# The output's store gets a semaphore of its own, awaited behind the context's closing, and sends 128 rows in place of 32

## The chip, the cores and the metric

The kernel runs on one core of one Trainium2 chip. The metric is the device time of one execution in microseconds (us). A profiled execution gives, beside its own time, a span: the time from the first to the last instruction of the program.

## The reference

One decode step (one token for each of two batch rows, D = 512) of a transformer block with adaptive layer norm:

```python
mod = (silu(c) @ w_mod)                  # six vectors sa, ca, ga, sb, cb, gb
h = layernorm(x) * (1 + ca) + sa
x = x + ga * attention(h)                # 32 heads of 128, caches K and V of 4096 rows each
h = layernorm(x) * (1 + cb) + sb
x = x + gb * mish_ffn(h)                 # 512 -> 1376 -> 512, Mish between
return x                                 # float32, 2 x 1 x 512
```

Everything is float32. The two caches are 2 x 32 x 4096 x 128 each, 134 MB a piece; with the weights the core reads 297 MB from HBM in one execution. The result is 4 KB.

## The kernel before

**The stream.** All that is read in bulk passes through three buffers called `room` (64 KB on each of 128 partitions). `stream()` (line 31) fixes by hand what each fill holds: for most fills one head of K and one head of V, with the pieces of `wq`, `wo` and the modulation weights fitted between. `load(n)` (line 134) issues the DMAs of fill n at line 141, all on the SyncE queue (SP in the profile); `used(...)` (line 146) calls it as soon as the buffer of fill n-3 is no longer needed. There are 45 such DMAs, in program order, and each SP instruction waits on semaphores for the buffer that it overwrites.

**The heads.** For every head VectorE multiplies K with the broadcast query (line 318), sums over the head dimension (line 321) and takes a row maximum; ScalarE makes the exponentials (line 337); TensorE sums V with those weights (line 359) and projects (line 390).

**The end.** After the last head come the second layer norm, the two layers of the feed-forward part (lines 514 and 556), the scaling with the last modulation vector (line 564), and the residual (line 565), whose result stands in the tile `y`, 128 partitions of 128 floats. Only eight of the 128 rows of `y` are part of the answer: every sixteenth row; the rest is padding that the matmul layout leaves. Line 566 stores every fourth row, 32 rows of 512 bytes, to the DRAM tensor `out`, as the last DMA of the SP queue:

```python
y = work.tile([P, P], F32, tag="sq", name="y", bufs=1)
nc.vector.tensor_tensor(out=y, in0=yps[:, :P], in1=mod[5], op=ALU.mult)
nc.vector.tensor_tensor(out=y, in0=y, in1=x2, op=ALU.add)
nc.sync.dma_start(out=out, in_=y[::OUT_STEP, :])
```

**The closing.** The kernel is built inside a `tile.TileContext` (line 636), which assigns the semaphores. When the context ends, it adds a closing of its own, whose instructions the profile files under line 636. SP waits, in six small semaphore instructions, for the full count of every semaphore that the context gave out: those of the DMAs (eight of them, taken in turn by all DMAs, the store too), and one of each engine. Then SP drains; all five engines meet at a barrier that POOL (GpSimd) leads; POOL drains and clears the context's semaphores; a second barrier follows, and the program of the kernel is over. The barriers use two semaphores that are not the context's.

The host takes every fourth of the 32 rows (line 639).

Of the kernel before, what the change touches and what calls it, by code (L numbers as in the profile page):

```python
# [8 lines left out]
F32 = mybir.dt.float32  # L9
# [4 lines left out]
P = 128  # L14
# [8 lines left out]
    "k": BIG, "v": HALF, "wq": W, "wo": W, "m01": 2 * W, "m2": W, "m3": W, "m4": W, "m5": W,  # L23
    "w1": 4 * sum(WIDTHS), "w2": 512 * len(CHUNKS),
}
OUT_STEP = 4
AHEAD = (14, 22)
ROW = 2 * BIG

# [40 lines left out]
def kernel(  # L70
# [3 lines left out]
    head: bass.AP,  # L74
    b1c: bass.AP,
    out: bass.AP,
):


# [6 lines left out]
    nc = tc.nc  # L86
# [16 lines left out]
    work = ctx.enter_context(tc.tile_pool(name="work", bufs=2))  # L103
# [42 lines left out]
    def used(*keys):  # L146
# [24 lines left out]
        out=fold, in_=ident.rearrange("p (g r) -> p r g", g=G), axis=AX.X, op=ALU.add  # L171
# [3 lines left out]
        out=mean_w, in0=fold[:, None, :].to_broadcast([P, G, R]), scalar1=1.0 / D, scalar2=None, op0=ALU.mult  # L175
# [4 lines left out]
        out=half, in_=ident.rearrange("p (b r) -> p r b", b=B), axis=AX.X, op=ALU.add  # L180
# [373 lines left out]
    for n in range(NCH):  # L554
        for t in range(G):
# [4 lines left out]
                start=(n == 0),  # L560
                stop=(n == NCH - 1),
            )
    y = work.tile([P, P], F32, tag="sq", name="y", bufs=1)
    nc.vector.tensor_tensor(out=y, in0=yps[:, :P], in1=mod[5], op=ALU.mult)  # L564
    nc.vector.tensor_tensor(out=y, in0=y, in1=x2, op=ALU.add)
    nc.sync.dma_start(out=out, in_=y[::OUT_STEP, :])


def _lay_out(np, a):
# [70 lines left out]
```

## Time and profile before

| | |
|---|---|
| time before, median of 3 runs | 698.54 us (698.48 to 698.58) |
| the profiled execution's own time | 698.42 us |
| its span, first to last instruction | 696.6 us |
| mean granted TensorE clock | 0.676 |
| VectorE (DVE) busy | 587.7 us, 84% of the span |
| TensorE (PE) busy | 283.8 us, 41% |
| read from HBM, written | 297.22 MB, 0.02 MB |
| mean rate of the DMA engines | 427 GB/s |

How to read it: the page names instructions by line of the kernel and engine, and tiles as output<-input. A `q` after an engine (SPq, POOLq) is its sequencer, which issues DMAs and handles semaphores; such instructions are not counted as busy time. Where a semaphore instruction waits, its row begins only when the wait is over. The chain of waits follows the work that ended last back from the last instruction; it ends at the last instruction that does work, and the closing and the store's flight are not in it. Times in the rows of the timeline are the start, in us from the span's start, and the duration.

### The profile page before, as it was taken

The page shows a single profiled execution, that of the slowest core. Times are in us where ns is not written, and L with a number is a line of the kernel's source. Part 1 is how long each engine was busy: PE and PEld are TensorE (multiplying, and loading weights), DVE is VectorE, ACT ScalarE, POOL GpSimd, SP SyncE. Part 2 cuts the span into 40 slices and gives each one's busy share as a digit, 9 for nine tenths or more (in the row PEclk, how much of TensorE's full clock was granted, in tenths as well). Part 3 has the DMA queues.
Part 4 walks back from the last instruction along what each step waited for, and adds up shares of the span by engine and source line. Part 5 has one row for each costly group of instructions (what it writes and reads, how often), then busy time and mean ns, then how long its engine had stood idle before and what let it go on. Part 6 is the DMA issues. An engine that isn't in the chain of part 4 may idle for free.

```text
span 696.6 us, 3912 instructions
## 1 busy us (share of the span) xinstructions
PE 283.8 (41%) x1636; PEld 102.4 (15%) x1636; DVE 587.7 (84%) x220; ACT 44.0 (6%) x168; POOL 4.2 (1%) x19
## 2 busy tenths in 40 slices
PE   3403334335245615335232806234333526224686
PEld 1200001001011201102100301011101101001234
DVE  3799899999999999999999999999999999899002
ACT  1000000000000000000000000000000000000010
POOL 2000000000000000000000000000000000000000
PEclk9855666667566665656585756666575657555789
DMA  9999999999999999999999999999999999999996
GB/s 392 452 421 421 426 474 421 419 429 421 467 422 425 429 425 456 429 425 426 433 448 429 426 429 437 440 430 429 433 437 437 429 425 422 452 427 420 423 422 270
DMA packets 6706, 297.49 MB, mean 427 GB/s; under 512 B 888, under 2 KB 928, under 8 KB 1184
## 3 DMA queue, kind: packets, MB, share of 16 engines
q1 hardware_dynamic: 6528, 297.23, 98.9%
q8 instruction: 13, 0.21, 0.1%
q10 hardware_dynamic: 160, 0.01, 0.0%
q14 instruction: 5, 0.04, 0.0%
HBM read 297.22 MB, written 0.02 MB: 427 GB/s over the span
## 4 chain that ended last, share of the span: by engine, by line
DMA 69%; DVE 28%; PE 2%; issue 0%; SPq 0%; ACT 0%; DVEq 0%
DMA room<-in_load 69%; DVE room L318 14%; DVE s L321 14%; PE ov L359 1%; PE qps L291 1%; PE modps L247 1%; PE yps L556 0%; SPq L141 0%; DVE m L334 0%; DVE hcw L280 0%; ACT q L292 0%; PE hps L237 0%; DVE y L564 0%; DVE hq L270 0%; DVE hq L271 0%
## 5 line engine op out<-in xcount | busy, mean ns | idle before, releaser
L318 DVE TENSOR_TENSOR room<-room,q 128x8192 f32<-128x8192 f32 x32 | 278.2, 8692 | 46.8 <-DMA room<-in_load 42.4
L321 DVE TENSOR_REDUCE s<-room 128x64 f32<-128x8192 f32 x32 | 277.9, 8683 | 0.4 <-DVE m L334 0.3
L359 PE MATMUL ov<-room,e 128*32 128x512 f32 x1024 | 176.4, 842 | 80.1 <-ACT e L337 63.9
L330 PE MATMUL mt<-d,same 128*128 128x64 f32 x64 | 18.2, 378 | 195.8 <-DVE d L328 195.8
L359 PEld LDWEIGHTS ov<-room,e 128*32 128x32 f32 x1024 | 39.2, 145 | 188.6 <-issue 133.8
L337 ACT ACTIVATE e<-s,m 64x64 f32<-64x64 f32 x64 | 22.1, 345 | 556.6 <-DVE m L334 555.8
L330 PEld LDWEIGHTS mt<-d,same 128*128 128x128 f32 x64 | 13.1, 254 | 225.8 <-DVE d L328 179.3
L291 PE MATMUL qps<-room,hcw 128*128 128x512 f32 x64 | 43.4, 844 | 4.8 <-DMA room<-in_load 4.0
L345 PE MATMUL l<-l,ones 128*128 128x8 f32 x16 | 4.6, 358 | 75.1 <-ACT e L337 75.1
L382 PE MATMUL otp<-pick,o 128*128 128x8 f32 (+2 forms) x72 | 13.4, 313 | 33.9 <-ACT o L374 32.0
L291 PEld LDWEIGHTS qps<-room,hcw 128*128 128x128 f32 x64 | 16.8, 274 | 26.4 <-issue 20.5
L374 DVE COPY o<-ov 128x256 f32<-128x256 f32 x1 | 0.4, 425 | 22.6 <-ACT o L374 22.6
L382 PEld LDWEIGHTS otp<-pick,o 128*128 128x128 f32 x72 | 12.6, 263 | 42.3 <-ACT o L374 39.4
L345 PEld LDWEIGHTS l<-l,ones 128*128 128x128 f32 x16 | 3.8, 296 | 76.5 <-ACT e L337 76.5
L334 DVE TENSOR_REDUCE m<-mt 128x1 f32<-128x64 f32 x32 | 6.9, 217 | 7.6 <-PE mt L330 7.6
L390 PE MATMUL att<-room,ot 128*32 128x512 f32 x62 | 10.1, 709 | 5.2 <-DMA room<-in_load 4.7
L337 ACT ACTIVATION_READ_ACCUMULATOR e<-s,m 64x1 f32 x64 | 11.8, 185 | 0.0
L328 DVE TENSOR_SCALAR d<-half,m 128x64 f32<-128x64 f32 x32 | 8.1, 254 | 1.1
L247 PE MATMUL modps<-room,ct 128*32 128x128 f32 (+1 forms) x160 | 8.1, 346 | 2.3 <-DMA room<-in_load 2.2
L326 DVE TENSOR_REDUCE m<-s 128x1 f32<-128x64 f32 x32 | 7.0, 217 | 0.9
L374 ACT COPY o<-ov 128x512 f32<-128x512 f32 (+1 forms) x9 | 5.0, 561 | 25.9 <-PE ov L359 25.7
L247 PEld LDWEIGHTS modps<-room,ct 128*32 128x32 f32 x160 | 5.0, 121 | 4.6 <-issue 4.4
(101 smaller groups left out, 60.6 us busy)
## 6 DMA issues: line engine op xcount, KB each, us to landing
room<-in_load SPq DMA_DIRECT2D x4, 4096.0 KB, 25.0
room<-in_load SPq DMA_DIRECT2D x1, 7168.0 KB, 39.1
room<-in_load SPq DMA_DIRECT2D x1, 3072.0 KB, 26.2
room<-in_load SPq DMA_DIRECT2D x3, 1024.0 KB, 28.3
room<-in_load SPq DMA_DIRECT2D x1, 2400.0 KB
room<-in_load SPq DMA_DIRECT2D x1, 2304.0 KB, 20.4
room<-in_load SPq DMA_DIRECT2D x1, 1376.0 KB, 15.8
room<-in_load SPq DMA_DIRECT2D x2, 256.0 KB, 22.8
```

What stands on the lines that cost most here:

```text
L247: nc.tensor.matmul(ps[R * g : R * (g + 1)], lhsT=ct[:, k, :], rhs=t[:, k, :].rearrange("p (m n) -> p m n", m=n)[:, :, P * g : P * (g + 1)] ...
L291: nc.tensor.matmul(ps, lhsT=hcw[:, k, :], rhs=wq_t[ch][:, k, :], start=(k == 0), stop=(k == G - 1))
L318: nc.vector.tensor_tensor(out=k_t[h], in0=k_t[h], in1=qv, op=ALU.mult)
L321: nc.vector.tensor_reduce(out=s_t[h], in_=k_t[h], axis=AX.X, op=ALU.add)
L326: nc.vector.tensor_reduce(out=m_t[h][:, 0:1], in_=s_t[h], axis=AX.X, op=ALU.max)
L328: nc.vector.tensor_scalar(out=d, in0=half, scalar1=m_t[h][:, 0:1], scalar2=None, op0=ALU.mult)
L330: nc.tensor.matmul(mps[h], lhsT=same, rhs=d, start=True, stop=True)
L337: nc.scalar.activation(e_t[i][own_b, :, M * i + 4 * b : M * i + 4 * b + 4], s_t[h][own_b].rearrange("p (c m) -> p c m", m=4), AF.Exp, bias ...
L345: nc.tensor.matmul(lps[n], lhsT=ones, rhs=sum_t[n % 2], start=True, stop=True)
L359: nc.tensor.matmul(ov[bank][R * g : R * (g + 1), :], lhsT=e_t[h % HC][:, NB // 2 * part + c, :], rhs=v_t[h, part][:, c, :], start=(first a ...
L382: nc.tensor.matmul(tps[:, x], lhsT=o_t[m], rhs=pick_t[n][:, m, x], start=(m == 0), stop=(m == 3),)
L390: nc.tensor.matmul(att[R * i : R * (i + 1), :], lhsT=ot_t[n % 2][:, i, :], rhs=wo_t[n][:, i, :], start=(n == 0), stop=(n == H // HC - (2 i ...
```

## The change

`OUT_STEP` goes from 4 to 1, so the store sends all 128 rows of `y` (64 KB in place of 16 KB, 128 rows of 512 bytes in place of 32), and the DRAM tensor `out` has 128 rows. The host takes every sixteenth.

The store adds to a semaphore `out_done` that is allocated outside of the context. Its name is put into `no_tile_sem_insts`, so the context neither counts it on one of its own semaphores nor waits for it. Behind the context's closing, SP waits until `out_done` has its 16 counts, and clears it.

`y` is allocated outside of the context's pools, since it is read after the context's last wait; it no longer shares the buffer of the tag `sq`.

```diff
-OUT_STEP = 4
+OUT_STEP = 1
...
+    out_done,
+    y,
...
-    y = work.tile([P, P], F32, tag="sq", name="y", bufs=1)
     nc.vector.tensor_tensor(out=y, in0=yps[:, :P], in1=mod[5], op=ALU.mult)
     nc.vector.tensor_tensor(out=y, in0=y, in1=x2, op=ALU.add)
-    nc.sync.dma_start(out=out, in_=y[::OUT_STEP, :])
+    store = nc.sync.dma_start(out=out, in_=y[::OUT_STEP, :]).then_inc(out_done, 16)
+    tc.no_tile_sem_insts.add(store.ins.name)
...
+    args["out_done"] = nc.alloc_semaphore("out_done")
+    args["y"] = nc.alloc_sbuf_tensor("y", [P, P], F32).ap()
     with tile.TileContext(nc) as tc:
         tile_adaln_decode_kernel(tc, **args)
+    nc.sync.wait_ge(args["out_done"], 16)
+    nc.sync.sem_clear(args["out_done"])
```

In the program as it is built, every engine has the same instructions in the same order as before, but for SP: the store waits for VectorE alone (before, it also waited for the DMA that had used its semaphore last), and one instruction stands behind the closing, which waits for `out_done` and clears it. One more thing differs there: each of the 45 loads carries a mark of the build for a prepared form of DMA (`ant_dge_precooked`), which the store of 32 rows with a stride of four lacked and the store of 128 rows has. All 201 SBUF tiles but five stand 512 bytes higher on each partition, because `y` lies below them.

## The prediction

> **What bounds the kernel now.** I read the page first (span, slices, chain), then the chain in order of time, then the rows of the stretch that the change touches: the last 3 us.
>
> ```profile
> span 696.6 us, 3912 instructions
> DMA  9999999999999999999999999999999999999996
> DMA room<-in_load 69%; DVE room L318 14%; DVE s L321 14%; PE ov L359 1%; PE qps L291 1%; PE modps L247 1%; PE yps L556 0%; SPq L141 0%; DVE m L334 0%; DVE hcw L280 0%; ACT q L292 0%; PE hps L237 0%; DVE y L564 0%; DVE hq L270 0%; DVE hq L271 0%
> ```
>
> The DMA engines are busy in every slice but the last, and the stream's loads hold 69% of the chain. The reader is to see two things: the time is set by a stream that the diff does not edit, and the store (line 566) is not even named in the chain. So a gain can come only from what follows the last arithmetic. That end, from four views (timeline, SP's instructions of line 566 and of 636, SP's waits):
>
> ```profile
> 693.74 0.29 DVE L565 TENSOR_TENSOR y<-y,x 128x128 f32<-128x128 f32 x1
> 694.06 0.55 SPq L566 DMA_DIRECT2D out<-y  x1
> L566 SPq DMA_DIRECT2D out<-y x1: 547/547/547, 694.1 to 694.1; - x1
> out<-y SPq DMA_DIRECT2D x1, 16.0 KB, 1.7
> ...
> L636 SPq EVENT_SEMAPHORE  x5: 17/28/28, 694.7 to 694.9; - x5
> L636 SPq EVENT_SEMAPHORE  x1: 27/27/27, 695.8 to 695.8; - x1
> L636 POOLq EVENT_SEMAPHORE_RANGE_CLEAR  x1: 96/96/96, 696.2 to 696.2; - x1
> L636 PEldq EVENT_SEMAPHORE  x1: 51/51/51, 696.6 to 696.6; - x1
> ...
> SPq L636 <- DMA out<-y: 0.9, 1, 0.9
> SPq L636 <- PEq L636: 0.6, 2, 0.4
> ```
>
> The store is issued at 694.06 and lands 1.7 us later, at 695.8. Of the closing's six semaphore instructions on SP five pass at once, at 694.7 to 694.9, and the sixth stands for 0.9 us until the store has landed (its row starts when the wait is over). Only then come the two barriers and POOL's clearing, and the last instruction of all is PE leaving the second barrier at 696.6. The flight is cut up by a view of the DMA packets and by one of stretches:
>
> ```profile
> GB/s 0 0 26 154 128 103 103 103 103 77 0 26 0 0 0 0 0 0 0 0 0 0 0 0 0 0 0 0 0 0 0 0 0 0 0 0 0 0 0 0
> DMA packets 48, 0.02 MB, mean 21 GB/s; under 512 B 16, under 2 KB 48, under 8 KB 48
> ...
> 694.60:695.25 0.65, 0.00 (x0) 0.00 (x0) 0.00 (x0) 0.00 (x0) 0.00 (x0) 1.00 0.00 0
> 695.25:695.46 0.21, 0.00 (x0) 0.00 (x0) 0.00 (x0) 0.00 (x0) 0.00 (x0) 1.00 0.30 78
> 695.46:695.80 0.34, 0.00 (x0) 0.00 (x0) 0.00 (x0) 0.00 (x0) 0.00 (x0) 1.00 0.00 0
> 695.80:696.63 0.83, 0.00 (x0) 0.00 (x0) 0.00 (x0) 0.00 (x0) 0.00 (x0) 0.69 0.00 0
> ```
>
> The first row has 40 slices of 0.02 us from 695.2. So the end before is a sum: issue 0.55 (to 694.61), silence 0.64 (to 695.25), packets 0.21 (32 with data and 16 of under 512 B, which are the counts), silence 0.34 until the counts are in (695.80), closing 0.83 (to 696.63).
>
> **The change part by part.**
>
> *The closing goes beside the flight.* In the built program the store adds to `out_done` alone, so all six of SP's semaphore instructions pass at once. The five took from 694.61 (the issue's end) to 694.93, 0.32 us; the rest of the closing takes 0.83 from the sixth on, as before. That work is not shortened; it is hidden beside the flight as long as the flight is longer.
>
> *The issue.* The 32-row store took 547 ns to issue. The built program marks the 128-row store as it marks the loads, so the nearest rows are the loads' issues, and, for the same two kinds on the other queue, ScalarE's two:
>
> ```profile
> L141 SPq DMA_DIRECT2D room<-in_load x31: 327/328/428, 118.9 to 643.9; - x31
> 1.07 1.15 ACTq L161 DMA_DIRECT2D cx<-in_head  x1
> 2.26 0.36 ACTq L164 DMA_DIRECT2D bias<-in_b1c  x1
> ```
>
> A marked load that waited takes 327 or 328 ns, one that follows another up to 428. On ScalarE the unmarked DMA (8 rows) took 1.15, the marked one (128 rows) 0.36. The store waits for VectorE, so I take 0.33: issue end at 694.06 + 0.33 = 694.39, a gain of 0.22. The bounds are 0.33 and, if the mark does nothing, 0.55.
>
> *The flight.* I keep the silence of 0.64 after the issue; the very first load, on an idle queue, agrees:
>
> ```profile
> 0.73 0.39 SPq L141 DMA_DIRECT2D room<-in_load  x1
> DMA  0000000099999009009090990000000000000009
> DMA packets 14, 0.46 MB, mean 573 GB/s; under 512 B 0, under 2 KB 0, under 8 KB 0
> ```
>
> Its issue ended at 1.12, and in this row (slices of 0.02 us from 1.6) the first packet is at 1.76: 0.64 again. So the first packet of the new store is at 695.03. Then it has 128 data packets in place of 32, eight in place of two on each of 16 engines. No row shows such a store, so I bound it from both sides. Low: in the stretch of 0.21 us the engines were busy 0.30 of it, 0.30 x 0.21 x 16 = 1.01 us of engine time, at most 1.01 / 32 = 0.032 us per data packet, so six more in file on an engine add 0.19. Nothing makes it less, since bytes and packets only grow. High: the 16 engines might start late one after the other, as in the load above, whose 14 first packets are spread over 0.6 us; then the last engine starts at +0.6 and needs 8 x 0.032 = 0.26, together 0.86 in place of 0.21, that is +0.65. The store's own 16 engines started closely (in the first five slices of its row), so I take a value near the low end, +0.25. The silence of 0.34 until the counts are in stays: landing at 695.03 + 0.21 + 0.25 + 0.34 = 695.83, about where it was. The shorter issue pays for the added rows.
>
> The Trainium skill, "DMA: Bandwidth & Descriptors", section "Anatomy of one DMA", puts a DMA at some 2.0 us fixed, mostly the write's receipt, plus bytes over 436e9 per second; by that the added 48 KB would be an estimated 0.11 us, and the sum 0.14 us better than mine. It speaks for the low end; the trace's flight of 1.7 us is somewhat shorter than its constant. The same page's section "Bandwidth", under "Measured", speaks against the change: about 10.5 ns a packet for a transfer of small packets, by which 96 more would be an estimated 1.0 us, and all of the gain would be lost (the second rival has this outcome). This trace does not agree with that rate: 48 packets went in 0.21 us, 4.4 ns each.
>
> *The wait behind the closing.* SP is through the closing at 694.39 + 0.32 + 0.83 = 695.54, and the other engines too, 0.29 before the landing. The wait then holds SP until 695.83. Behind it on SP stands only the clearing, and no engine waits for that. Its price: before, SP's own semaphore row took 0.03, and POOL's clearing 0.10, so 0.13 at most and 0.02 at least; I take 0.13. End of the span: 695.96. If the flight were shorter than expected, the cover of 0.29 would be gone and the closing would set the end, at 695.54, so the span cannot fall by more than about 1.0 us here.
>
> *The rest.* The wait of the store for an older DMA goes:
>
> ```profile
> SPq L566 <- DMA room<-in_load: 1.4, 1, 1.4
> SPq L566 <- DVE y L565: 22.2, 1, 22.2
> ```
>
> It was over 22.2 us before the store could start, so it costs nothing either way. `y` outside of the pools removes no instruction and no wait on VectorE, whose order is unchanged; lines 564 and 565 keep 0.29 each. The other edits are on the host or only move tiles by 512 bytes.
>
> *The sum.* Span: 696.63 - 695.96 = 0.67 us less; with the ends of the transfer 0.73 and 0.27. Around the span lie 698.42 - 696.6 = 1.8 us that no row shows. If what comes after the program starts when the last engine (now SP) is through, they stay: 0. If an engine other than SP is the slow one there, it now starts up to 696.63 - 695.54 = 1.09 earlier rather than 0.67: up to 0.42 more. I take 0.1, nearer to none. In all 0.77 against the profiled 698.42, that is 697.65; the median of the runs shown is 0.12 higher, so 697.77 against it, rounded **697.8**.
>
> **The rivals.**
>
> 1. *The store's wait is not moved, only doubled.* If the context still awaited the store, the closing would stay behind the landing (695.83 + 0.83) and the new wait would add 0.13: 696.79, +0.16, about 698.7. Against it: in the built program the store has left the context's semaphores, and SP's closing has no count for it. For it: the rows of before show only that the wait exists.
>
> 2. *The landing is late; the wait behind the closing takes the place of the one removed.* This one ends slower than before. It decides from the point where the landing passes 696.63 - 0.13 = 696.50, that is, when the flight after the shorter issue grows by over 0.92 us (695.58 would be the landing without added rows). Price: if the silence of 0.34 us before the counts are in grew with the data, four times as long, it would add 1.02, with 0.19 for the packets 1.21: landing at 696.79, end at 696.92, +0.29, about 698.8. For it: the silence is longer than the packets themselves, so something other than the packets sets it. Against it: every engine's packets go out together, and one silence followed all 32.
>
> 3. *The stream pays for the moved tiles.* With nearly every tile 512 bytes higher and a larger output in DRAM, the loads may run at another rate, either way. The stream is 69% of 696.6, 481 us, and its rate is not the same everywhere:
>
> ```profile
> 160.00:260.00 100.00, 42.48 (x180) 13.33 (x178) 92.90 (x28) 6.32 (x24) 0.00 (x0) 0.65 1.00 434
> 460.00:560.00 100.00, 41.97 (x184) 15.70 (x188) 93.00 (x28) 6.93 (x26) 0.00 (x0) 0.64 1.00 432
> ```
>
> A step from 434 to 432 GB/s, 0.46%, over 481 us is 2.2 us: about 700.0 the one way, 695.6 the other. It makes the kernel slower than before from a loss of 0.77 / 481 = 0.16%. For it: the engines are full (share 1.00), so nothing would hide it. Against it: neither the sizes of the loads nor their order changes, and 434 and 432 stand in one execution with fixed tiles, so that difference has another cause.
>
> 4. *More falls than the span shows*: the other engines' earlier end shortens what follows the program by the whole 0.42, and the transfer is at its low end: 0.73 + 0.36 = 1.09 (the floor of the other engines' gain), about 697.4.
>
> **How the numbers follow.** Forecast (697.5 to 698.4) 0.78; rival 4 (697.3 to 697.5) 0.10; rival 1 at 698.7 0.02; rival 2 at 698.8 0.05; rival 3 0.05, split 0.03 slower and 0.02 faster. The range goes from the largest gain, 1.1, with the runs' own spread of 0.1, to the smallest, 0.27, with the same spread: 697.3 to 698.4. It leaves out rivals 1 to 3, 0.12. A measurement of this kernel can tell about 0.2% from no change, 1.4 us; the forecast and rivals 1, 2 and 4 lie within it, so same 0.95, faster 0.02, slower 0.03.
>
> **What would show each step.** Right: SP's issue of the store at about 330 ns; SP's six semaphore rows of the closing all within some 0.4 us of it; POOL's clearing at 695.2, ahead of the landing; 144 packets on the store's queue from about 695.0; landing 1.7 to 1.8 us after the issue starts; SP's last instruction, not PE's, ending the span at about 696.0, and the stream's rows unchanged to 0.1 us. Wrong: an issue of 550 ns (the mark does nothing, 0.22 less gain); first packets spread over more than 0.3 us or a silence longer than 0.34 (rival 2, in whole or in part); the closing still behind the landing (rival 1); a start of line 565 off 693.74 by over 0.3 us (rival 3); a time outside of the span other than 1.8 us (rival 4).

## The result and the profile after

The changed kernel takes 697.59 us in the median (22 runs, 697.27 to 697.79). The kernel before, run beside it, takes 698.63 (22 runs, 698.36 to 699.03). The ratio is 0.9985 with a 95% interval of 0.9979 to 0.9991. That is 1.04 us or 0.15% faster: less than the 0.2% below which the prediction calls two times the same, but the interval does not reach 1, so the gain is real. The profiled execution takes 697.51 us, its span is 695.7.

The end of the changed kernel in the timeline:

```profile
693.47 0.29 DVE L565 TENSOR_TENSOR y<-yps,mod 128x128 f32<-128x128 f32 x1 [2.78 <-PE yps L558]
693.79 0.29 DVE L566 TENSOR_TENSOR y<-y,x 128x128 f32<-128x128 f32 x1
694.11 0.34 SPq L567 DMA_DIRECT2D out<-y  x1
```

The last addition starts at 693.79 in place of 693.74, so to 0.05 us the stream has neither gained nor lost in these two executions. The issue is down from 0.55 to 0.34. Then SP's waits, in which the 0.9 for the store is gone:

```profile
SPq L567 <- DVE y L566: 23.5, 1, 23.5
SPq L640 <- PEq L640: 0.6, 2, 0.4
```

The instructions of the closing (line 640 here) in three of its stretches: its six semaphore instructions, POOL's clearing, the last barrier.

```profile
L640 SPq EVENT_SEMAPHORE  x6: 17/28/28, 694.5 to 694.8; - x6
...
L640 POOLq EVENT_SEMAPHORE_RANGE_CLEAR  x1: 96/96/96, 695.2 to 695.2; - x1
...
L640 POOLq EVENT_SEMAPHORE  x2: 17/17/17, 695.4 to 695.5; - x2
...
L640 PEldq EVENT_SEMAPHORE  x1: 51/51/51, 695.6 to 695.6; - x1
```

All six pass at once, at 694.5 to 694.8, and POOL clears at 695.2 in place of 696.2. PE leaves the last barrier at 695.6 in place of 696.6. The new instruction behind the closing:

```profile
L643 SPq EVENT_SEMAPHORE_RANGE_CLEAR  x1: 25/25/25, 695.7 to 695.7; - x1
```

And the flight, cut at the issue's end (694.45), the first and last packet and the landing:

```profile
694.45:694.94 0.49, 0.00 (x0) 0.00 (x0) 0.00 (x0) 0.00 (x0) 0.00 (x0) 1.00 0.00 0
694.94:695.30 0.36, 0.00 (x0) 0.00 (x0) 0.00 (x0) 0.00 (x0) 0.00 (x0) 1.00 0.62 182
695.30:695.66 0.36, 0.00 (x0) 0.00 (x0) 0.00 (x0) 0.00 (x0) 0.00 (x0) 1.00 0.00 0
```

The reader is to see that the landing has hardly moved, 695.8 before and 695.66 now, with four times the data, while the closing has moved from behind it to beside it: it ends within 0.1 us of the landing.

**The table of all runs.** The "tail" is the profiled execution's own time less the start of its last addition (the row `y<-y,x`), which takes the stream's differences between executions out. SP and POOL "through" are the starts of their last rows in the span.

| kernel | median us | before beside it | ratio, 95% interval | tail us | POOL through | SP through |
|---|---|---|---|---|---|---|
| before | 698.63 | | | 4.68 | 696.5 | 696.6 |
| changed | 697.59 | 698.63 | 0.9985 (0.9979 to 0.9991) | 3.72 | 695.5 | 695.7 |
| own_sem_32rows | 697.88 | 698.65 | 0.9988 (0.9979 to 0.9997) | 3.82 | 695.7 | 695.9 |
| rows128_only | 698.32 | 698.65 | 0.9995 (0.9986 to 1.0004) | 4.47 | 696.8 | 696.9 |
| y_moved_only | 698.58 | 698.65 | 0.9998 (0.9989 to 1.0007) | 4.79 | 696.6 | 696.7 |
| own_sem_32_contiguous | 697.65 | 698.65 | 0.9985 (0.9976 to 0.9993) | 3.75 | 695.6 | 695.7 |
| four_copies | 698.42 | 698.67 | 0.9997 (0.9988 to 1.0006) | 4.41 | 696.0 | 697.0 |
| eight_copies | 699.16 | 698.67 | 1.0008 (0.9999 to 1.0016) | 5.24 | 695.9 | 697.8 |
| wait_on_pool | 697.68 | 698.67 | 0.9987 (0.9978 to 0.9996) | 3.84 | 696.1 | 695.9 |
| store_on_act | 697.31 | 698.67 | 0.9981 (0.9973 to 0.9990) | 3.43 | 695.6 | 696.1 |
| eight_copies_pool | 699.79 | 698.57 | 1.0018 (1.0009 to 1.0027) | 5.80 | 697.7 | 695.8 |
| changed_again | 697.58 | 698.57 | 0.9985 (0.9976 to 0.9994) | 3.60 | 695.8 | 695.9 |
| store_on_act_again | 697.26 | 698.57 | 0.9981 (0.9972 to 0.9990) | 3.45 | 695.3 | 695.7 |

The tails of one kernel differ by about 0.1 us between executions (changed 3.72 and 3.60; before and y_moved_only, whose ends are alike, 4.68 and 4.79). What lies outside of the span, the time less the span, is on average over the runs 1.83 us in before, 1.76 in changed, 1.75 in own_sem_32rows, 1.38 in four_copies, 1.36 in eight_copies, 1.87 in wait_on_pool, 1.89 in eight_copies_pool, and 1.46 and 1.47 in the two of store_on_act.

### The profile page after: what moved, and what is told of

It is laid out like the page before. It is cut to its first block, busy times and chain, and to the rows that moved or that the text cites. A ratio compares the mean times of both kernels' runs of the same rounds, so it can differ in the third digit from the quotient of the medians.

```text
span 695.7 us, 3912 instructions
## 1 busy us (share of the span) xinstructions
PE 284.7 (41%) x1636; PEld 103.9 (15%) x1636; DVE 587.5 (84%) x220; ACT 44.0 (6%) x168; POOL 4.2 (1%) x19
## 2 busy tenths in 40 slices
DMA packets 6802, 297.54 MB, mean 428 GB/s; under 512 B 888, under 2 KB 1024, under 8 KB 1280
## 4 chain that ended last, share of the span: by engine, by line
DMA 69%; DVE 28%; PE 3%; issue 0%; SPq 0%; ACT 0%; DVEq 0%
DMA room<-in_load 69%; DVE room L320 14%; DVE s L323 14%; PE qps L293 1%; PE ov L361 1%; PE modps L249 1%; PE yps L558 0%; SPq L143 0%; DVE m L336 0%; DVE hcw L282 0%; PE hps L239 0%; ACT q L294 0%; DVE hq L272 0%; DVE hq L273 0%; DVE y L565 0%
## 5 line engine op out<-in xcount | busy, mean ns | idle before, releaser
L361 PE MATMUL ov<-room,e 128*32 128x512 f32 x1024 | 174.1, 832 | 74.2 <-ACT e L339 40.4
L293 PE MATMUL qps<-room,hcw 128*128 128x512 f32 x64 | 46.1, 891 | 4.8 <-DMA room<-in_load 4.0
L294 ACT ACTIVATE q<-qps 128x512 f32<-128x512 f32 x8 | 4.8, 597 | 15.9 <-PE qps L293 15.7
```

What stands on the lines that cost most here:

```text
L293: nc.tensor.matmul(ps, lhsT=hcw[:, k, :], rhs=wq_t[ch][:, k, :], start=(k == 0), stop=(k == G - 1))
L361: nc.tensor.matmul(ov[bank][R * g : R * (g + 1), :], lhsT=e_t[h % HC][:, NB // 2 * part + c, :], rhs=v_t[h, part][:, c, :], start=(first a ...
```

## The experiments

Theory 1: the gain is the closing that now goes beside the flight; the time follows the end of the closing, and SP's wait behind it is covered by something on another engine after the program. Theory 2: the time follows the landing and SP's last instruction. Rival 3: the gain lies in the store's form, not in the semaphore.

### The parts alone

The changed kernel with

```diff
-OUT_STEP = 1
+OUT_STEP = 4
```

> The semaphore of its own and the wait behind the closing alone; the store keeps 32 rows with a stride of four (OUT_STEP 4). Theory 1 (the gain comes from the closing going beside the flight; the time follows the end of the closing): the issue stays at 0.55 us, the closing ends 1.16 us behind the issue's end, at about 695.8, and the time is 0.85 below before: 697.8. Theory 2 (the time follows the landing and SP's last instruction): landing at 695.8, SP through at 695.85, 0.78 below before: 697.85. Rival 3 (the gain is the shorter issue and flight of the marked 128-row store): no gain, 698.6.

Measured 697.88, 0.77 below before. Its timeline and its closing:

```profile
693.81 0.29 DVE L566 TENSOR_TENSOR y<-y,x 128x128 f32<-128x128 f32 x1
694.13 0.55 SPq L567 DMA_DIRECT2D out<-y  x1
```

```profile
L640 SPq EVENT_SEMAPHORE  x8: 17/28/28, 694.7 to 695.8; - x8
L640 POOLq EVENT_SEMAPHORE  x4: 17/17/17, 695.2 to 695.7; - x4
```

The issue stays at 0.55 and most of the gain is there, so rival 3 falls. Theories 1 and 2 lie too near each other here to be told apart.

The other part is the kernel before with

```diff
-OUT_STEP = 4
+OUT_STEP = 1
```

> Only OUT_STEP 1: 128 rows, the context's own semaphore, the closing behind the landing as before. Theories 1 and 2: the issue falls to 0.34, the silence behind it to 0.50, the packets take some 0.2 longer, landing 0.16 earlier, and the whole time by as much: 698.5. Rival 3 (all of the gain is in the store's form): 697.6.

Measured 698.32, 0.33 below before, with an interval that takes in no change; the tail is 0.21 shorter (4.47 against 4.68). Rows of its timeline, and of SP's waits:

```profile
694.26 0.29 DVE L565 TENSOR_TENSOR y<-y,x 128x128 f32<-128x128 f32 x1
694.58 0.35 SPq L566 DMA_DIRECT2D out<-y  x1
```

```profile
SPq L636 <- DMA out<-y: 0.9, 1, 0.9
```

The closing still stands for 0.9 us behind the store. (This execution's last addition was at 694.26, half a microsecond later than before's: that is the stream, and why the tail is the better measure.) The two parts alone, 0.77 and 0.33, make 1.10; together they gave 1.04.

The place of `y` alone, before with

```diff
-    y = work.tile([P, P], F32, tag="sq", name="y", bufs=1)
...
+    args["y"] = nc.alloc_sbuf_tensor("y", [P, P], F32).ap()
```

> Only the place of y: allocated outside of the pools, so that nearly all tiles stand 512 bytes higher; the store and the closing as before. All three theories: 698.6, within 0.1. The rival that the moved tiles change the stream: another start of the last addition than 693.7 to 693.8, and a time that differs by as much.

Measured 698.58, and the last addition starts where it did within 0.1:

```profile
693.83 0.29 DVE L565 TENSOR_TENSOR y<-y,x 128x128 f32<-128x128 f32 x1
```

The moved tiles cost nothing that can be seen.

### Form or number of rows

```diff
-    store = nc.sync.dma_start(out=out, in_=y[::OUT_STEP, :]).then_inc(out_done, 16)
+    store = nc.sync.dma_start(out=out, in_=y[:32, :]).then_inc(out_done, 16)
```

> As the changed kernel, but the store sends the first 32 rows, without a stride; it leaves three quarters of the rows unsent, so the answer is not the reference's. It has the build's mark. If the mark sets the issue's length: 0.34, landing some 0.16 earlier than with 128 rows, about 695.5. If the number of rows sets it: 0.55, landing at 695.8. Theory 1: the time follows the closing, so with the short issue 697.6, as the changed kernel, though the landing is earlier. Theory 2: 697.45, earlier by what the landing gains.

Measured 697.65. Its issue, SP's clearing and its flight; last, for comparison, the flight of own_sem_32rows, with the same 32 rows and the stride:

```profile
694.17 0.36 SPq L567 DMA_DIRECT2D out<-y  x1
...
L643 SPq EVENT_SEMAPHORE_RANGE_CLEAR  x1: 25/25/25, 695.7 to 695.7; - x1
```

```profile
694.53:695.02 0.49, 0.00 (x0) 0.00 (x0) 0.00 (x0) 0.00 (x0) 0.00 (x0) 1.00 0.00 0
695.02:695.25 0.23, 0.00 (x0) 0.00 (x0) 0.00 (x0) 0.00 (x0) 0.00 (x0) 1.00 0.30 72
695.25:695.60 0.35, 0.00 (x0) 0.00 (x0) 0.00 (x0) 0.00 (x0) 0.00 (x0) 1.00 0.00 0
```

```profile
694.68:695.32 0.64, 0.00 (x0) 0.00 (x0) 0.00 (x0) 0.00 (x0) 0.00 (x0) 1.00 0.00 0
695.32:695.53 0.21, 0.00 (x0) 0.00 (x0) 0.00 (x0) 0.00 (x0) 0.00 (x0) 1.00 0.30 78
```

So the form, not the number of rows, sets the issue (0.36 against 0.55) and the silence behind it as well (0.49 against 0.64). Whether it is the build's mark or the missing stride these two runs cannot say, since they go together. The two runs with copies below, which have neither the mark nor a stride over the partitions, have the long form (0.64 at the issue, 0.63 and 0.64 behind it), so the missing stride alone does not make it short. The landing is about 0.1 earlier relative to the issue than with 128 rows, and the time does not follow it: 697.65 against 697.59. That does not tell the theories apart, though theory 2 was expected at 697.45: the landing, at 695.60, is ahead of SP's clearing, so it is the closing that holds SP here, and SP is through 1.9 us behind the start of the last addition (693.85), as in the changed kernel.

### How much of SP's wait is covered

The landing is made late, with the closing kept: every row is sent four or eight times, to a larger output.

```diff
-    store = nc.sync.dma_start(out=out, in_=y[::OUT_STEP, :]).then_inc(out_done, 16)
+    store = nc.sync.dma_start(out=out, in_=y[:, None, :].to_broadcast([P, 4, P])).then_inc(out_done, 16)
```

> As the changed kernel, but the store sends every row four times, to four rows of a larger output: 512 rows of 512 bytes. It has no mark, so the issue is 0.55 or longer, as with 32 rows and a semaphore of its own, and the closing ends where it does there, about 695.8. 32 packets on each engine at 0.027 us each: landing at about 696.6. Theory 1 in its strong form (SP's wait is covered by what follows the program on other engines, by some 0.2 to 0.4 us): 698.2 to 698.4. Theory 2 (SP's last instruction sets the time): 0.8 later than with 32 rows, 698.6.

> As four_copies, with eight copies of each row: 64 packets on each engine, landing at about 697.5. Both theories: 0.86 more than four_copies, since any cover is used up there; theory 1 about 699.2, theory 2 about 699.5. What tells them apart is the distance of this line from the time with 32 rows and a semaphore of its own.

Measured 698.42 and 699.16. In four_copies SP's clearing comes at 697.0:

```profile
L643 SPq EVENT_SEMAPHORE_RANGE_CLEAR  x1: 25/25/25, 697.0 to 697.0; - x1
```

In eight_copies POOL's last row of the closing is at 695.9 and SP's clearing at 697.8:

```profile
L640 POOLq EVENT_SEMAPHORE  x4: 17/17/17, 695.4 to 695.9; - x4
```

```profile
L643 SPq EVENT_SEMAPHORE_RANGE_CLEAR  x1: 29/29/29, 697.8 to 697.8; - x1
```

The span of these kernels ends with SP's clearing. From own_sem_32rows to four_copies its median grows by 0.9 us (696.1 to 697.0), and the time by only 0.54. From four to eight copies the span grows by 0.8 and the time by 0.74. So there is a cover of some 0.4 us, used up by four copies. The sizes show where: outside of the span, four_copies has 698.38 - 697.0 = 1.38 and eight_copies 699.12 - 697.8 = 1.32, while before, changed and own_sem_32rows have 1.7 to 1.8. What follows SP's last instruction takes 1.3 to 1.4 us when SP is alone late; with all engines through together something else is late.

Which engine it is, two runs ask, the first with the ordinary store, the second with eight copies:

```diff
-    nc.sync.wait_ge(args["out_done"], 16)
-    nc.sync.sem_clear(args["out_done"])
+    nc.gpsimd.wait_ge(args["out_done"], 16)
+    nc.gpsimd.sem_clear(args["out_done"])
```

> As the changed kernel, but POOL waits for out_done and clears it, in place of SP. Theory 1, strong form (POOL is the engine that is late in what follows the program): POOL is through at 695.75 in place of 695.53, so 0.2 later than the changed kernel: 697.8. Theory 2: the last instruction is at 695.75 as on SP, so 697.6.

> As eight_copies, with the wait and the clearing on POOL in place of SP; the landing, at about 697.7, is so late that nothing covers the wait. If what follows the program takes longer on POOL than on SP (theory 1, strong form: outside of the span eight_copies had 1.32 us, the changed kernel, with the last work hidden behind POOL's, 1.81), about 0.4 to 0.5 above eight_copies: 699.6. Theory 2: the same as eight_copies, 699.2.

The first gave 697.68, between the two expectations and no verdict by itself; its tail is 0.12 to 0.24 longer than the changed kernel's two. The second settles it, 699.79 in place of 699.16, though its last instruction stands 0.1 us earlier than the one on SP:

```profile
L643 POOLq EVENT_SEMAPHORE_RANGE_CLEAR  x1: 44/44/44, 697.7 to 697.7; - x1
```

Outside of the span it has 699.56 - 697.7 = 1.86, where eight_copies had 1.32. What follows POOL's last instruction takes half a microsecond longer than what follows SP's. So the end is the later of two: POOL's last row + about 1.9, and SP's last row + 1.3 to 1.4. Taken with the ends of these rows and with 1.92 and 1.37, this rule meets the time of all thirteen profiled executions to within 0.1 us.

The changed kernel by this rule: POOL is through at 695.5, which makes 697.4 to 697.5; SP at 695.7, which makes 697.0 to 697.1. POOL's side is the later one (697.51 measured), and the wait for the store is covered with about 0.4 to spare. One thing is not shown: PE, DVE and ACT leave the same barrier within 0.1 us of POOL, and no run made one of them late alone, so one of them may take as long there as POOL. Either way it is the end of the closing that sets the time, and not SP's wait behind it. The Trainium skill, "Runtime: NRT & Kernel Launch", section "The ~15µs preamble/postamble breakdown", says that behind the kernel stands a barrier in which every engine is awaited, then resets and a second barrier. A late engine that sets the time agrees with that. Its figures for these steps add up to some 5 us; what lies outside of the span here is below 2 in all, and whether the measured time takes in every one of these steps no run shows.

### A version that is faster still

If the time follows the closing, the closing can be started earlier: SP goes into it while ScalarE issues the store.

```diff
-    store = nc.sync.dma_start(out=out, in_=y[::OUT_STEP, :]).then_inc(out_done, 16)
+    store = nc.scalar.dma_start(out=out, in_=y[::OUT_STEP, :]).then_inc(out_done, 16)
```

> As the changed kernel, but ScalarE's queue issues the store; SP still waits for it behind the closing. SP enters the closing when VectorE is done, and ScalarE when it has issued, at about 694.5, so the closing ends 0.35 to 0.4 earlier, at about 695.2; the landing stays at about 695.7. Theory 1: between 697.2 and 697.4, faster than the changed kernel by 0.2 to 0.4. Theory 2: the landing is unchanged, so 697.6.

> The changed kernel once more, beside the next one on the same chip: 697.6 in both theories.

> The store on ScalarE's queue once more. Theory 1: 0.3 below the changed kernel, 697.3. Theory 2: as the changed kernel, 697.6.

Measured 697.31, and beside the changed kernel on one chip 697.26 (697.10 to 697.51) against 697.58 (697.35 to 697.81), 11 runs each. The tails are 3.43 and 3.45 against 3.72 and 3.60. Of store_on_act_again the timeline, the closing with SP's clearing, and SP's waits:

```profile
693.80 0.29 DVE L566 TENSOR_TENSOR y<-y,x 128x128 f32<-128x128 f32 x1
694.13 0.36 ACTq L567 DMA_DIRECT2D out<-y  x1
```

```profile
L640 POOLq EVENT_SEMAPHORE  x4: 17/17/17, 694.7 to 695.3; - x4
L640 PEldq EVENT_SEMAPHORE  x2: 51/51/51, 694.8 to 695.3; - x2
...
L643 SPq EVENT_SEMAPHORE_RANGE_CLEAR  x1: 25/25/25, 695.7 to 695.7; - x1
```

```profile
SPq L640 <- DVE y L566: 2.4, 1, 2.4
...
SPq L643 <- DMA out<-y: 0.4, 1, 0.4
```

SP waits for VectorE inside the closing, the closing ends at 695.3 in place of 695.6, and the landing stays, so that SP now waits for it 0.4 us and is through at 695.7, as in the changed kernel. The time falls by 0.3, as the closing, and not by none, as the landing: theory 2, which fell with eight_copies_pool, falls here a second time. By the rule above SP's side is 695.7 + 1.35 = 697.05 and POOL's 695.3 + 1.9 = 697.2, so the cover is nearly used up: the next gain would have to shorten both.

## Why the prediction was right, and which term was off

*What bounds the kernel.* Right: the stream is untouched, and all of the difference lies behind the last addition (tail 4.68 against 3.72 and 3.60).

*The closing beside the flight.* Right, and it is most of the gain: 0.77 alone. The forecast put the closing's end at 695.54; PE's last row is at 695.6.

*The issue.* Right: 0.33 was taken, 0.34 measured. With the shorter silence, less the longer packets, it is worth 0.2 to 0.3 alone (rows128_only).

*The flight.* Two of its terms were too long, and the errors add up. The silence behind the issue was taken at 0.64, for which the very first load seemed to agree; it is 0.49 in this form. Why the load, which is marked too, has 0.64 no run shows; it reads from HBM, and own_sem_32_contiguous shows that the store's silence goes with the store's form. The packets were taken at +0.25 and took +0.15 (0.36 against 0.21). That is under the low end of 0.19, below which "nothing makes it less": from two to eight packets an engine added 0.025 us for each, not 0.032. Landing 695.66 in place of 695.83, or, behind the start of the last addition, 1.87 in place of 2.09: 0.15 from the silence, 0.10 from the packets, less 0.03 from the issue and the counts. The two figures of the Trainium skill quoted in the prediction ("DMA: Bandwidth & Descriptors", "Anatomy of one DMA" and "Measured") stand there for DMAs that GpSimd issues, the second for loads from HBM; this store leaves SBUF by SP's queue, so neither is made for it. Of the two estimates worked out from them, 0.11 us for the added bytes lies near the +0.15 measured, and 1.0 us for the added packets does not.

*The clearing.* Taken at up to 0.13, it is 0.03: SP's own clearing takes 25 ns, where POOL's of twelve semaphores takes 96.

*The rest of the span.* Taken as 0.1 of at most 0.42, "nearer to none". This is where the mechanism was off: the sum was made up to SP's last instruction as if it set the time, and what lies outside of the span was left almost as it was. As an entry of the sum the 0.1 even came out: 1.83 us lie outside of the span before and 1.76 in the changed kernel, 0.07 less, while the span fell by 0.9 in place of 0.67, because the flight and the clearing were shorter than forecast. That agreement is luck. If SP had been through as late as forecast, at 695.96, POOL's side of the rule above would still have set the time, near 697.4 to 697.5, and the term would have had to be 0.3 to 0.4. By this rule the gain is that of the closing's end, about 1.0, and neither the landing nor the wait nor the silence counts at all in the changed kernel. Measured 1.04 against 0.77 forecast. The outcome lies between the forecast and rival 4 (1.09), whose mechanism, that engines other than SP end earlier and set the time, is the one that holds; its other half, a transfer near the low end, does not count.

*The rivals.* 1: no count for the store in the closing, and no wait (SP's waits above). 2: the landing did not come late; the silence of 0.34 before the counts is 0.36 with four times the data, and 0.35 in eight_copies with 32 times as much:

```profile
695.47:697.42 1.95, 0.00 (x0) 0.00 (x0) 0.00 (x0) 0.00 (x0) 0.00 (x0) 0.58 0.94 269
697.42:697.77 0.35, 0.00 (x0) 0.00 (x0) 0.00 (x0) 0.00 (x0) 0.00 (x0) 0.50 0.00 0
```

So it did not grow with the data from 16 KB to 512 KB. 3: nothing that can be seen, by y_moved_only (698.58 against 698.65). 4: see the rest of the span.

What stays open: what follows the program on POOL and takes the half microsecond, since no view shows it, and whether PE, DVE or ACT take as long there; and whether the mark itself, or something else that goes with it, makes the store's form short.

## What to carry to other kernels

A wait for the last store in front of a closing that all engines share puts the store's flight and the closing end to end; given a semaphore of its own and awaited behind the closing, the two lie side by side, and the shorter one is free. Ask then which engine is the last in what follows the program, not which instruction is the last in the span: here a wait on SP was covered by some 0.4 us, and with the store of eight copies the same wait cost 0.63 us more on POOL than on SP. A store's form is worth a look too: 128 rows without a stride landed 1.5 us after the start of the issue, 32 rows with one 1.7 us, because issue and silence gained more than the added packets cost.

## What the runs showed of the hardware that was not expected

A store in the prepared form (with the build's mark) was shorter twice: 0.34 to 0.36 us in place of 0.55 at the issue, and 0.49 in place of 0.64 from the issue's end to the first packet. A store of 1024 rows of 512 bytes took 1.95 us for its packets, 64 on each of 16 engines, 0.030 us a packet; eight on each took 0.36. The time from the last packet to the last count was 0.34 to 0.36 us in every store that was cut up here, from 16 KB to 512 KB. And what follows the program took about 1.9 us behind POOL's last instruction where POOL was late alone (eight_copies_pool), and 1.3 to 1.4 us behind SP's where SP was (four_copies, eight_copies).
